# A decode step fed by one stream of weights and caches: the packed array in sixteen lines instead of 128

## The chip, the cores and the metric

The kernel runs on one core of a Trainium2 chip. The metric is the device time of one execution in microseconds (us); less is better. The runs before the change took 375.45, 376.38 and 376.48 us, median 376.38 us.

## The reference: what is computed

One decode step for a batch of two tokens, in float32. The token vector is normalised; one branch is attention over the last 2,048 positions of a key and value cache (32 heads of 128), the other a gated feed-forward block without a nonlinearity. Both are added to the input.

```python
B, D, H, Dh, Sk, F = 2, 512, 32, 128, 8192, 1376
W = min(4096, max(256, Sk // 4))                 # 2048
xn = layernorm(x)
q = (xn @ wq) per head
p = softmax(q . k_cache[:, :, Sk-W:] * Dh**-0.5)
attn = (p . v_cache[:, :, Sk-W:]) @ wo
ffn = ((xn @ w_gate) * (xn @ w_up)) @ w_down
out = x + attn + ffn
```

With one query per head, every byte of cache and weight is used once: the kernel reads 159.47 MB and does little arithmetic with each byte.

## The kernel before, in words

The host packs all inputs but x into one array in device memory, `stream`. It has 128 lines, one for each partition of the on-chip memory; a line holds, load after load, what that partition is to receive. A load is one DMA: it takes a stretch of every line and writes it to the same columns of all 128 partitions of one on-chip tile, `ring` (called `step` in the profile, as the DRAM array is called `in_stream_dram`). `lines()` computes at which element of a line each load starts (a multiple of 128 elements) and how long a line is; its length in units of 128 elements is kept odd. `placed()` gives the column range of each load in `ring`, `loads()` the list of loads.

There are 26 loads. Two small ones, x0 and x1, bring the gate, up and first query weights. Then keys and values of four heads at a time (k0, v0, k1, v1, ...), each 16,384 elements of each partition; between them w1 and w4 with the down-projection, query and output weights. The tail is seven smaller loads: v28, v30, v31, d0, wo7, d1 and d2. All are issued by SyncE (SP), in that order, by `issue(name)`. Keys always go to one region of `ring` and values to another, so the load of the next group's keys waits until TensorE has read the present keys (`issue(f"k{g + 1}")` stands behind `scores(g)`), and likewise for values (behind the loop over `weigh`). While one of the two regions is being read, the load for the other is in flight.

The loop over eight head groups g runs: the query projection (`project`, tile q_ps), the scores (`scores`, s_ps), the maxima and exponentials (`maxima`, `weights`), the weighted values (`weigh`, o_ps), the gathering of heads (`gather`) and the output projection (`wo`, acc). TensorE's program is a hardware loop with waits on semaphores; a load adds 16 to its semaphore when all of it has landed. Every operation is recorded through one helper, so nearly all rows of the profile carry its line, L133.

Of the kernel before, what the change touches and what calls it, by code (L numbers as in the profile page):

```python
# [10 lines left out]
P = 128  # L11
# [41 lines left out]
def loads():  # L53


    v, k = [("v", h) for h in range(H)], [("k", h) for h in range(H)]
    pair = [(("wq", g), ("wo", g - 1)) for g in range(NG)]
    wd = {i: ("wd", i) for i in range(NFC + 1)}
    last = H - HG
    out = {  # L60
        "x0": (None, C_GU, [("gu", GU[0])]),
        "x1": (None, C_GU + GU[0][1], [("gu", GU[1]), ("c", 0)]),
        "k0": ("K", C_K, k[:HG]),
        "v0": ("V", C_V, v[:HG]),
        "w1": (
            None, C_Q[1] - (len(EARLY) - 1) * D - REST,
            [wd[i] for i in EARLY] + [*pair[3], *pair[2], *pair[1]],
        ),
    }
    for g in range(1, NG - 1):  # L70
        out[f"k{g}"] = ("K", C_K, k[g * HG : g * HG + HG])
        out[f"v{g}"] = ("V", C_V, v[g * HG : g * HG + HG])
        if g == 3:
            out["w4"] = (None, C_W, [*pair[4], *pair[7], *pair[6], *pair[5]])
    out["k7"] = ("K", C_K, k[last:])
    halves = [("half", (h, b)) for h in range(last, H) for b in range(B)]
    for name, a, b in (("v28", 0, 4), ("v30", 4, 7), ("v31", 7, 8)):
        out[name] = ({0: "V", 4: "V2", 7: "V3"}[a], C_V + a * W, halves[a:b])
    at = C_K
    for name, ids in (("d0", ROWS), ("wo7", None), ("d1", STRIPS[:-1]), ("d2", STRIPS[-1:])):  # L80
        if ids is None:
            out[name] = ("wo", C_O, [("wo", NG - 1)])
            continue
        out[name] = (None, at, [wd[i] for i in ids])
        at += len(ids) * D
    return out
# [10 lines left out]
def placed():  # L97


    got, spans = {}, {}  # L100
    for name, (_, at, fields) in loads().items():
        lo = at
        for kind, i in fields:
            got[kind, i] = (at, width(kind, i))
            at += width(kind, i)
        spans[name] = (lo, at)
    return got, spans


LINE = 128  # L110


def lines():


    starts, at = {}, 0
    for name, (lo, hi) in placed()[1].items():
        starts[name] = at
        at += -(-(hi - lo) // LINE) * LINE
    return starts, at + LINE * (1 - at // LINE % 2)  # L120


# [320 lines left out]
def build(nc, stream, x_nat, out):  # L443
# [44 lines left out]
    got = {key: ring[:, c : c + w] for key, (c, w) in where.items()}  # L488
    src, tag_of = {}, {}
    starts, total = lines()  # L490
    rows = stream.rearrange("(p i) -> p i", i=total)
    for name, (tag, _, _) in loads().items():
        lo, hi = spans[name]
        src[name] = rows[:, starts[name] : starts[name] + hi - lo]
        tag_of[name] = tag

    def issue(name):
# [30 lines left out]
    total, var, std, rstd = (st[:B, i : i + 1] for i in range(4))  # L528
# [177 lines left out]
    for g in range(NG):  # L706
# [17 lines left out]
        if g == 0:  # L724
# [7 lines left out]
            for i in range(3):  # L732
                part = slice(32 * i, 32 * i + 32)
# [39 lines left out]
def laid_out(x):  # L773

    import numpy as np

    a = x["A_x"].reshape(B, D)
    rows = np.arange(P)
    c = np.zeros((P, CX), a.dtype)
    for n in range(N):  # L780
        c[:, n] = rows % 32 // 4 == n
    for i in range(4):
        c[:, N + i] = rows % 4 == i
        c[:, N + 4 + i] = rows == 32 * i
    for b in range(B):
        c[:, N + 8 + b] = rows % 32 == b
    k, v = (x[name][:, :, SK - W :, :] for name in ("A_k_cache", "A_v_cache"))
    wq = x["A_wq"].reshape(NC, P, H * DH)
    wo = x["A_wo"].reshape(NG, HG, P, D)
    first = [x[name].reshape(NC, P, F) for name in ("B_w_gate", "B_w_up")]  # L790
    first = np.concatenate(first + [wq[:, :, :FB]], axis=2)
    first = np.pad(first, ((0, 0), (0, 0), (0, RUNS * GW - WIDE)))
    wd = x["B_w_down"]

    def field(kind, i):
        if kind == "c":
            return c
        if kind == "half":
            return field("v", i[0])[:, i[1] * W : (i[1] + 1) * W]
        if kind == "k":  # L800
            return k[:, i].transpose(2, 0, 1).reshape(P, CK)
        if kind == "v":
            blocks = v[:, i].reshape(B, NJ, NK, 32, DH)
            return blocks.transpose(1, 3, 0, 2, 4).reshape(P, CK)
        if kind == "wq":
            return wq[:, :, i * FB : (i + 1) * FB].transpose(1, 0, 2).reshape(P, NC * FB)
        if kind == "wo":
            return wo[i].transpose(1, 0, 2).reshape(P, HG * D)
        if kind == "wd":
            w = wd[i * P : (i + 1) * P]  # L810
            if i < NFC:
                return w
            return np.concatenate(
                [w[:, :REST], w[:, REST:].reshape(3, 32, P).transpose(1, 0, 2).reshape(32, REST)]
            )
        runs = first.reshape(NC, P, RUNS, GW).transpose(1, 2, 0, 3).reshape(P, -1)
        return runs[:, i[0] : i[1]]

    starts, total = lines()
    stream = np.zeros((P, total), a.dtype)  # L820
    for name, (_, _, fields) in loads().items():
        at = starts[name]
        for kind, i in fields:
            part = field(kind, i)
            stream[:, at : at + part.shape[1]] = part
            at += part.shape[1]
    return {"stream": stream.ravel(), "x": a}


# [25 lines left out]
```

## Time and profile before

| | |
|---|---|
| median of three runs | 376.38 us |
| the profiled execution's own time | 375.21 us |
| its span on the core | 373.8 us |
| TensorE (PE) busy | 215.1 us, 58% |
| VectorE (DVE) busy | 62.7 us, 17% |
| the loads' DMA queue (q1) busy | 98.9% of 16 DMA engines' span |
| bytes read | 159.47 MB |

The span is what the profiler saw between the first and the last instruction; the execution's own time is 1.41 us longer. "q1" is the queue on which SP's DMAs run, spread over 16 DMA engines; its share is the time that packets took on the sixteen, so 100% means that all sixteen worked all the time. The chain of work that ended last is followed back from the last instruction; "DMA" in it is time in which the chain waited for a load to land.

### The profile page before, as it was taken

To read this page: it belongs to the slowest core of one execution; us is meant where nothing else is said; L and a number is where in the kernel's file an instruction comes from. 1 tells how busy PE (TensorE), PEld (TensorE's weight loads), DVE (VectorE), ACT (ScalarE), POOL (GpSimd) and SP (SyncE) were. 2 spreads that over 40 slices of the span, in tenths; PEclk is the share of its full clock that TensorE was granted. 3 is DMA by queue.
4 is the path that set the end of the run, shared out by engine and by line. 5 is a ranking of instruction groups with operands and counts; after the bars stand their busy time and mean duration, and the time that the engine had idled before them with its cause. 6 is when DMAs were issued, how large, how long until landed. Compare 5 with 4: busy or idle time off the path is not lost.

```text
span 373.8 us, 3210 instructions
## 1 busy us (share of the span) xinstructions
PE 215.1 (58%) x1362; PEld 53.4 (14%) x1362; DVE 62.7 (17%) x161; ACT 15.9 (4%) x31; POOL 15.5 (4%) x38
## 2 busy tenths in 40 slices
PE   0688770097828780776154414637662877095765
PEld 0011110022102110221011100102110211021221
DVE  3000141012120212021202010202120122003203
ACT  5011110000000000000000000000000000000000
POOL 2000000022000200000000200000200020000000
PEclk9989997568986898699869585859896889689999
DMA  8999899999899999989999999899999989999996
GB/s 335 495 449 442 365 428 491 427 449 435 358 442 449 449 449 449 449 351 435 449 449 449 449 449 414 372 449 449 449 449 449 442 365 428 449 449 393 435 419 276
DMA packets 3892, 159.54 MB, mean 427 GB/s; under 512 B 434, under 2 KB 562, under 8 KB 1076
## 3 DMA queue, kind: packets, MB, share of 16 engines
q1 hardware_dynamic: 3888, 159.54, 98.9%
q10 hardware_dynamic: 4, 0.00, 0.0%
HBM read 159.47 MB, written 0.07 MB: 427 GB/s over the span
## 4 chain that ended last, share of the span: by engine, by line
DMA 70%; PE 27%; DVE 1%; ACT 1%; issue 1%; SPq 0%; ACTq 0%
DMA step<-in_stream_dram 70%; PE o_ps L133 14%; PE q_ps L133 8%; PE s_ps L133 3%; PE acc L133 1%; ACT step L133 1%; PE tot L133 1%; DVE qt L133 1%; DVE red L133 0%; DVE om L133 0%; PE pk L133 0%; SPq L133 0%; ACT qz L133 0%; DVE oT L133 0%; ACTq L302 0%
## 5 line engine op out<-in xcount | busy, mean ns | idle before, releaser
L133 PE MATMUL o_ps<-step,p 128*32 128x512 f32 x512 | 71.5, 698 | 57.5 <-DMA step<-in_stream_dram 56.3
L133 PE MATMUL s_ps<-step,qz 128*8 128x512 f32 x512 | 60.6, 628 | 29.1 <-DMA step<-in_stream_dram 22.2
L133 PE MATMUL q_ps<-step,xn 128*2 x112 | 58.7, 674 | 16.5 <-POOL none L133 10.5
L133 PEld LDWEIGHTS o_ps<-step,p 128*32 128x32 f32 x512 | 17.0, 122 | 94.2 <-DMA step<-in_stream_dram 59.8
L133 PEld LDWEIGHTS s_ps<-step,qz 128*8 128x8 f32 x512 | 14.2, 93 | 75.6 <-issue 64.9
L133 POOL COPY step<-step 128x2048 f32<-128x2048 f32 x6 | 11.3, 1889 | 181.9 <-PE acc L133 181.9
L133 PEld LDWEIGHTS q_ps<-step,xn 128*2 128x2 f32 x112 | 9.9, 93 | 61.2 <-issue 61.2
L133 DVE TENSOR_REDUCE mt<-s_ps 128x1 f32<-128x512 f32 x8 | 5.5, 692 | 77.0 <-PE s_ps L133 77.0
L133 PE MATMUL acc<-step,oT 128*2 128x256 f32 x128 | 10.9, 469 | 11.6 <-POOL none L133 8.4
L133 DVE RECIPROCAL rec<-tot 128x8 f32<-128x8 f32 x8 | 1.7, 208 | 73.0 <-PE tot L133 73.0
L133 DVE TENSOR_TENSOR xr<-xr,acc 128x256 f32<-128x256 f32 (+1 forms) x17 | 7.4, 437 | 38.5 <-PE acc L133 38.4
L133 PE MATMUL acc<-step,hT 128*2 128x512 f32 (+1 forms) x10 | 3.3, 995 | 17.7 <-DMA step<-in_stream_dram 17.7
L133 DVE STREAM_TRANSPOSE qt<-q_ps 32x128 f32<-32x128 f32 x28 | 8.6, 306 | 24.8 <-PE q_ps L133 24.5
L133 DVE TENSOR_TENSOR om<-o_ps,cst 128x512 f32<-128x512 f32 x7 | 4.8, 691 | 36.8 <-PE o_ps L133 36.8
L133 PE MATMUL pk<-cst,red 128*128 128x8 f32 x16 | 3.3, 276 | 13.1 <-DVE red L133 13.1
L133 ACT COPY qz<-qt 128x8 f32<-128x8 f32 x8 | 1.6, 204 | 207.9 <-DVE qt L133 207.9
L133 PE MATMUL top<-dg,ones 128*128 128x32 f32 x16 | 3.3, 286 | 10.3 <-DVE dg L133 10.3
L133 ACT ACTIVATE p<-t,zero 128x128 f32<-128x128 f32 x8 | 4.2, 522 | 93.9 <-DVE t L133 93.9
L133 DVE TENSOR_REDUCE red<-om 128x128 f32<-128x512 f32 x7 | 7.1, 1019 | 0.2
L133 DVE TENSOR_TENSOR step<-step 2x1376 f32<-2x1376 f32 x1 | 1.6, 1580 | 32.2 <-ACT step L133 32.2
L133 POOL MEMSET none<- 128x1 f32 x18 | 1.6, 98 | 101.4 <-DMA step<-in_stream_dram 76.9
L133 DVE STREAM_TRANSPOSE sT<-s_ps 128x512 f32<-128x512 f32 x8 | 5.7, 709 | 0.0
(56 smaller groups left out, 55.6 us busy)
## 6 DMA issues: line engine op xcount, KB each, us to landing
step<-in_stream_dram SPq DMA_DIRECT2D x1, 7360.0 KB, 26.7
step<-in_stream_dram SPq DMA_DIRECT2D x1, 5590.5 KB, 17.4
step<-in_stream_dram SPq DMA_DIRECT2D x1, 4096.0 KB, 23.0
step<-in_stream_dram SPq DMA_DIRECT2D x1, 3072.0 KB, 27.7
step<-in_stream_dram SPq DMA_DIRECT2D x2, 1024.0 KB, 25.8
step<-in_stream_dram SPq DMA_DIRECT2D x1, 956.5 KB, 4.6
step<-in_stream_dram SPq DMA_DIRECT2D x1, 768.0 KB, 20.2
step<-in_stream_dram SPq DMA_DIRECT2D x1, 512.0 KB, 23.1
```

What stands on the lines that cost most here:

```text
L133: return getattr(engine, self.method)(*args, **self.kw)
```

## The change

The packed array gets 16 lines instead of 128. A line belongs to eight neighbouring partitions: line q to partitions 8q to 8q+7. Within a line, each load's eight partition rows lie directly behind each other; so a load takes from each line one run of eight rows without a gap. Before, the eight rows were each a line apart (311,680 elements). A load's start in a line is rounded up to 128 elements as before, and a line is 2,491,776 elements long. On the host side the array is filled accordingly. What lands where in `ring` is the same, and so are the number, order, sizes and waits of all loads.

```diff
-LINE = 128
+LINE, SHARE = 128, P // 16

 def lines():
     starts, at = {}, 0
     for name, (lo, hi) in placed()[1].items():
         starts[name] = at
-        at += -(-(hi - lo) // LINE) * LINE
+        at += -(-SHARE * (hi - lo) // LINE) * LINE
     return starts, at + LINE * (1 - at // LINE % 2)
...
     rows = stream.rearrange("(p i) -> p i", i=total)
     for name, (tag, _, _) in loads().items():
         lo, hi = spans[name]
-        src[name] = rows[:, starts[name] : starts[name] + hi - lo]
+        share = rows[:, starts[name] : starts[name] + SHARE * (hi - lo)]
+        src[name] = share.rearrange("q (n i) -> q n i", n=SHARE)
         tag_of[name] = tag
...
     starts, total = lines()
-    stream = np.zeros((P, total), a.dtype)
+    stream = np.zeros((P // SHARE, total), a.dtype)
     for name, (_, _, fields) in loads().items():
-        at = starts[name]
-        for kind, i in fields:
-            part = field(kind, i)
-            stream[:, at : at + part.shape[1]] = part
-            at += part.shape[1]
+        part = np.concatenate([field(kind, i) for kind, i in fields], axis=1)
+        part = part.reshape(P // SHARE, -1)
+        stream[:, starts[name] : starts[name] + part.shape[1]] = part
```

No instruction changes its place on any engine. What changes is the form of the 26 loads on SP. Here is the beginning of SP's program as a difference (- before, + after); the numbers are the destination's dimensions, and the three rows are the loads x0, x1 and k0.

```order
-L133 DMA step<-in_stream_dram 128x1913
-L133 DMA step<-in_stream_dram 128x11181
-L133 DMA step<-in_stream_dram 128x16384
+L133 DMA step<-in_stream_dram 128x1x1913
+L133 DMA step<-in_stream_dram 128x1x11181
+L133 DMA step<-in_stream_dram 128x1x16384
 L334 UNCONDITIONAL_BRANCH
```

Before, source and destination were both 128 rows by n elements. Now the source is 16 by 8 by n, and the destination, still 128 rows, gets a dimension of size one between them so that both sides have three. The other 23 loads change in the same way.

## The prediction

> **What bounds the kernel now.** I read the page's DMA part first, because the kernel uses every byte once.
>
> ```profile
> span 373.8 us, 3210 instructions
> PE 215.1 (58%) x1362; PEld 53.4 (14%) x1362; DVE 62.7 (17%) x161; ACT 15.9 (4%) x31; POOL 15.5 (4%) x38
> DMA packets 3892, 159.54 MB, mean 427 GB/s; under 512 B 434, under 2 KB 562, under 8 KB 1076
> q1 hardware_dynamic: 3888, 159.54, 98.9%
> DMA 70%; PE 27%; DVE 1%; ACT 1%; issue 1%; SPq 0%; ACTq 0%
> ```
>
> The loads' queue keeps sixteen DMA engines busy for 98.9% of 373.8 us, 369.7 us. No compute engine comes near that. The chain of waits agrees: 70% of it is waiting for loads, and its PE pieces run while the next load is already moving. So the kernel lasts as long as its DMA engines need for their bytes, and a change of their rate shows in full.
>
> Next, whether the rate has a ceiling. The table by stretches (columns: the stretch, its length, busy time of each engine, granted clock, DMA share, GB/s):
>
> ```profile
> 113.00:152.00 39.00, 23.73 (x158) 6.12 (x158) 6.53 (x17) 0.72 (x2) 2.08 (x3) 0.81 0.99 430
> 152.00:191.00 39.00, 21.94 (x162) 6.13 (x166) 6.53 (x17) 0.73 (x2) 0.00 (x0) 0.85 0.99 430
> 191.00:249.00 58.00, 25.60 (x162) 6.09 (x161) 6.53 (x17) 0.73 (x2) 2.22 (x5) 0.71 1.00 434
> 249.00:288.00 39.00, 23.24 (x162) 6.11 (x165) 6.53 (x17) 0.73 (x2) 2.09 (x3) 0.85 0.99 430
> 288.00:346.00 58.00, 37.83 (x254) 9.95 (x250) 10.68 (x27) 0.93 (x3) 2.08 (x3) 0.84 0.99 427
> ```
>
> Keys, values and weights land in these stretches, TensorE's load varies from 25.60 of 58 us to 37.83 of 58, and the rate stays between 427 and 434 GB/s: 430/16 = 26.9 GB/s for each engine. That is the signature of sixteen equal fixed lanes, all full, not of a memory that answers unevenly. Reads that come easier therefore have almost nothing to give, and lanes that are used less evenly have everything to take.
>
> **The change part by part.** Bytes, row lengths, destination columns, order and waits stay the same. The term is 0.
>
> Issuing. The three-dimensional form may take SP longer to decode.
>
> ```profile
> L133 SPq DMA_DIRECT2D step<-in_stream_dram x26: 327/328/433, 0.7 to 348.1; - x26
> 1.28 0.53 ACTq L133 DMA_DIRECT2D xr<-in_x_dram x1
> step<-in_stream_dram SPq DMA_DIRECT2D x16, 30.3
> step<-in_stream_dram SPq DMA_DIRECT2D x1, 956.5 KB, 4.6
> ```
>
> SP's 26 issues take 0.328 us (first row: minimum, median, maximum in ns). The dearest issue in this trace is ScalarE's, 0.53 us, so I bound the extra by 0 and 0.2 us each. A load of 8,192 KB (the x16 row) lands 30.3 us after its issue but takes 8.39 MB/430 = 19.5 us to move: it stands about 10.8 us behind another load, and 0.2 us disappears in that. Only the very first issue has no cover: +0.2 us at most, and 26 x 0.2 = 5.2 us if all cover were gone. I take 0.2. A wait is not added, so nothing new queues behind SP.
>
> Reading. Eight rows of a load now lie behind each other instead of 1.25 MB apart. What easier reads could give: x0, 956.5 KB, took 4.6 us to land where 0.98/0.430 = 2.3 us would do. Say all 2.3 us of that came from scattered first reads, which is generous since the same 4.6 us hold the issue and the landing signal: a gain of 0 to 2.3 us. A loss is possible too (sixteen long runs could meet in the memory); no row prices it. I take 0, because behind the start the sixteen lanes are full.
>
> Writing. This is the term that decides. A load is dealt out to the sixteen engines by the outermost rows of its two sides. Before, both sides had 128 rows, so any dealing that is the same on both sides was possible, also one that gives an engine partitions far apart. Now one side has 16 lines and line q holds partitions 8q to 8q+7, so an engine that is dealt a line must write eight neighbouring partitions. If the present dealing was already this one, nothing changes: 0. If it was chosen so that every engine has a way of its own into the on-chip memory, which the level 26.9 GB/s in every stretch suggests, then the new dealing can make two engines write through the same way at the same time while another way is empty. Two on one way of 26.9 GB/s get 13.5 each, and the 369.7 us of transfers become 739.4: +369.7 us. So the bounds are 0 and +369.7.
>
> [...]
>
> How long do two engines stay together? Both carry equal bytes in equal order. While they share, they advance alike, so the distance between them stays what it was at the start; it only helps as a share of half a load, 19.5/2 = 9.75 us. The start scatters by at most the 2.3 us above, 24% of 9.75. A load counts as landed when the slowest pair is done; with eight pairs spread evenly over 0 to 24%, the smallest distance is about 24/9 = 2.7%. I take that: 369.7 x 0.973 = 359.7 us.
>
> The sum, against the profiled execution's own time: 375.2 + 0.2 + 0 + 359.7 = 735.1 us. That execution lies 1.2 us below the median of the runs, 376.38, so I forecast 736 us. All computing hides: PE's 215.1 us fit twice over, and what follows the last landing stays:
>
> ```profile
> 370.76 0.04 issue
> 371.93 0.29 DVE red L133
> ```
>
> The last load lands at 370.76 of 373.8 us: 3.0 us behind it, already in the sum.
>
> **The rivals.** *The pairs drift apart.* If the sharing is not quite even, the distance within a pair grows until one engine writes its first half while the other writes its second; from then on nobody meets. For it: nothing holds them together. Against it: equal bytes, equal rates in every stretch above, and the slowest of eight pairs counts. At best one meeting is paid, 9.75 us: 375.2 + 0.2 + 9.75 = 385 us; at worst it ends where the forecast's own lower end lies, with the whole 24% head start: 375.4 + 0.76 x 369.7 = 656. The middle is 520.
>
> *No meeting: the same time.* The dealing stays what it was, or the ways into the memory are wider than an engine, or the sixteen share a pool that doesn't care who writes where. For it: the level rate would also come from engines that are themselves the limit. Then only 0.2 us of issuing is left: 375.4, or 376.6 as a median. It decides wherever two engines can pass one way at 26.9 GB/s each.
>
> *Faster.* Reading eight adjacent rows takes the start's scatter away: 375.2 - 2.3 = 372.9, or 374.1 as a median. Against it: the queue is at 98.9%, and 2.3 us is the whole of what x0 lost.
>
> **How the numbers follow.** Forecast 0.55, drifting apart 0.28, no meeting 0.14, faster 0.03. The rows show full lanes but not whose they are, hence the 0.14; that nearly two thirds of the rest goes to a lasting meeting follows from the equal rates. The time predicted is the forecast's 736 us, its own range 656 (the full head start) to 760 (the full 744.9 plus 2% for what sharing itself may lose). The range for 8 in 10 has to take in the drifting pairs down to their best, so it is 385 to 760; it leaves out no meeting, faster, and a little of the ends. A measurement of this kernel tells about 0.3% from no change: faster 0.03, same 0.13, slower 0.84 (0.01 of no meeting lies over that bound).
>
> **What would show it.** If right: the queue's share stays near 99% while the mean falls to about 217 GB/s; the stretches show 215 to 225 instead of 430; the sixteen large loads take about 60 us to land; the share of DMA in the chain of waits rises from 70% to about 85%, and PE's busy time stays at 215 us. Drifting pairs would show low GB/s in the early stretches and 430 in the late ones. No meeting: all rows above within a per cent, SP's issues alone longer. What would make it wrong is a way into the on-chip memory that takes two engines at once, or a dealing that still keeps engines apart.

## The result

The changed kernel takes 776.31 us, median of six runs (773.42 to 776.99), against 375.49 us before (median of six, 375.17 to 376.48): 2.066 times as long, 95% interval 2.063 to 2.069. The direction was as forecast, and so, as the experiments show, was the mechanism in the main. The time lies 16 us above the upper end of the range, 760 us, and 40 us above the forecast of 736.

The page of the changed kernel, the lines that answer to those of before:

```profile
span 775.2 us, 3210 instructions
PE 229.9 (30%) x1362; PEld 54.2 (7%) x1362; DVE 62.6 (8%) x161; ACT 15.9 (2%) x31; POOL 15.5 (2%) x38
DMA packets 3892, 159.54 MB, mean 206 GB/s; under 512 B 434, under 2 KB 562, under 8 KB 1076
q1 hardware_dynamic: 3888, 159.54, 99.4%
another core or an unknown queue 65%; PE 21%; DMA 10%; DVE 2%; issue 1%; ACT 0%; SPq 0%; POOL 0%; POOLq 0%; ACTq 0%
```

The number of packets and the bytes are the same to the last digit shown. The sixteen DMA engines are as busy as before, 99.4%, for twice as long: 770.5 us instead of 369.7, a factor of 2.084. The mean rate is 206 GB/s instead of 427. The chain of waits shows one weakness of such a view: most of the waits for loads now stand under "another core or an unknown queue", because the releaser was not matched. There is one core, and the loads are all that is waited for at those places; 65% and 10% together answer to the 70% of before.

The stretches show no ramp (columns as before: the stretch, its length, busy time of each engine, granted clock, DMA share, GB/s), and the issues and landings have their rows too:

```profile
40.00:200.00 160.00, 54.25 (x262) 11.55 (x264) 13.14 (x31) 5.44 (x10) 4.11 (x6) 0.68 0.99 204
200.00:360.00 160.00, 43.72 (x296) 10.99 (x288) 13.05 (x34) 1.45 (x4) 2.09 (x3) 0.66 1.01 209
360.00:520.00 160.00, 34.44 (x216) 8.10 (x212) 8.90 (x24) 1.25 (x3) 2.22 (x5) 0.61 0.99 204
520.00:680.00 160.00, 46.98 (x312) 11.67 (x304) 13.05 (x34) 1.45 (x4) 4.18 (x6) 0.66 1.02 210
L133 SPq DMA_DIRECT2D step<-in_stream_dram x26: 536/536/679, 0.7 to 725.4; - x26
step<-in_stream_dram SPq DMA_DIRECT2D x16, 72.4
```

204 to 210 GB/s from beginning to end: the pairs did not drift apart. An issue on SP takes 0.536 us instead of 0.328.

The trace also holds each DMA packet with its start, duration and size; a packet of 65,536 bytes here is one partition's row of one load (2,048 of them, 128 for each of the sixteen large loads). The records name neither the engine nor the partition; rows are put down to one engine where each starts as the one before it ends, and which partitions it writes is inferred. Rows that follow each other in this way, start in us and duration in ns:

```
before, rows of 65,536 bytes:  120.0:2418 122.4:2418 124.8:2418 127.2:2418 129.7:2418 132.1:2418 134.5:2418
after,  rows of 65,536 bytes:  100.0:5124 105.2:5111 110.3:5118
after,  w1, 58,880 bytes:      115.4:4415 119.8:4600 124.4:4594 129.0:4600 133.6:4422 138.0:4599 142.6:4598 147.2:4599
```

A row took 2.418 us; now most rows take 5.116 (the median of all 2,048 such rows), 2.12 times as long, and none took less than 4.935. In w1's eight rows the first and the fifth are a little quicker (4,415 and 4,422 ns among 4,594 to 4,600). If an engine writes eight neighbouring partitions, the fifth row is where it goes on from its first four to its next four: that would be the halves of a share, with which the forecast counts.

### The profile page after: what moved, and what is told of

The parts are those of the page before. It is cut to its first block, busy times and chain, and to the rows that moved or that the text cites. A ratio compares the mean times of both kernels' runs of the same rounds, so it can differ in the third digit from the quotient of the medians.

```text
span 775.2 us, 3210 instructions
## 1 busy us (share of the span) xinstructions
PE 229.9 (30%) x1362; PEld 54.2 (7%) x1362; DVE 62.6 (8%) x161; ACT 15.9 (2%) x31; POOL 15.5 (2%) x38
## 2 busy tenths in 40 slices
DMA packets 3892, 159.54 MB, mean 206 GB/s; under 512 B 434, under 2 KB 562, under 8 KB 1076
## 3 DMA queue, kind: packets, MB, share of 16 engines
q1 hardware_dynamic: 3888, 159.54, 99.4%
## 4 chain that ended last, share of the span: by engine, by line
another core or an unknown queue 65%; PE 21%; DMA 10%; DVE 2%; issue 1%; ACT 0%; SPq 0%; POOL 0%; POOLq 0%; ACTq 0%
DMA step<-in_stream_dram 10%; PE s_ps L133 6%; PE q_ps L133 6%; PE o_ps L133 6%; PE acc L133 1%; DVE red L133 1%; DVE mt L133 0%; DVE om L133 0%; ACT step L133 0%; PE top L133 0%; PE pk L133 0%; PE tot L133 0%; DVE qt L133 0%; DVE mtt L133 0%
## 5 line engine op out<-in xcount | busy, mean ns | idle before, releaser
L133 PE MATMUL o_ps<-step,p 128*32 128x512 f32 x512 | 75.3, 730 | 197.6 <-DMA step<-in_stream_dram 197.6
L133 PE MATMUL s_ps<-step,qz 128*8 128x512 f32 x512 | 71.3, 720 | 185.3 <-DMA step<-in_stream_dram 185.3
L133 DVE STREAM_TRANSPOSE qt<-q_ps 32x128 f32<-32x128 f32 x28 | 8.6, 306 | 24.8 <-PE q_ps L133 24.6
L133 PEld LDWEIGHTS acc<-step,oT 128*2 128x2 f32 x128 | 3.0, 91 | 37.6 <-POOL none L133 28.9
```

Of the source, the lines that this page charges most:

```text
L133: return getattr(engine, self.method)(*args, **self.kw)
```

## The experiments

**The dealing or the reading?** Theory 1 says that two engines write through one way (one entry into the on-chip memory) at the same time, because each is dealt eight neighbouring partitions. The rivals: long adjacent runs are slow to read, or the three-dimensional form of the loads is slow. Two kernels take the change apart. The first keeps adjacent rows and three dimensions, but in lines of four partitions:

```diff
-LINE, SHARE = 128, P // 16
+LINE, SHARE = 128, P // 32
```

> The array in 32 lines of four neighbouring partitions instead of 16 lines of eight; each load's rows are still adjacent within a line, and the loads are still three-dimensional. Theory 1 (two engines write through the same way into the on-chip memory at the same time because each is dealt eight neighbouring partitions): 32 lines can be dealt so that an engine gets two lines far apart, as in the kernel before, so about 375.5 us (375 to 377) and 430 GB/s in the stretches. Rival 2 (long adjacent runs are read more slowly): runs half as long, still far slower than before, 500 to 776. Rival 3 (the three-dimensional form of the loads is slow): 776.

The second keeps the old layout, in which nothing is adjacent, and changes the dealing alone:

```diff
-    rows = stream.rearrange("(p i) -> p i", i=total)
+    rows = stream.rearrange("(q i) -> q i", i=8 * total + LINE)[:, : 8 * total]
+    rows = rows.rearrange("q (n i) -> q n i", i=total)
...
-        src[name] = rows[:, starts[name] : starts[name] + hi - lo]
+        src[name] = rows[:, :, starts[name] : starts[name] + hi - lo]
...
+    stream = np.pad(stream.reshape(16, -1), ((0, 0), (0, LINE)))
```

> The old layout, every partition's row in a line of its own 1.25 MB from the next, but the loads described as 16 times 8 rows (a gap of 512 bytes after each eight lines keeps them so). Nothing is adjacent; only the dealing to the engines is that of the change. Theory 1: 776 us (765 to 785). Rival 2 (reading of adjacent runs): 375 to 377. Rival 3 (the form): 776 too, told apart by the run with 32 lines.

With 32 lines: 375.76 us, 1.0013 times the kernel before (1.0002 to 1.0023). With the old layout in sixteen shares: 774.29 us, 2.062 (2.059 to 2.066). Two stretches of each, 32 lines first, and the issues with 32 lines:

```profile
113.00:152.00 39.00, 22.91 (x158) 6.05 (x158) 6.53 (x17) 0.73 (x2) 2.08 (x3) 0.85 1.02 440
191.00:249.00 58.00, 25.40 (x158) 6.20 (x158) 6.53 (x17) 0.73 (x2) 2.22 (x5) 0.74 1.00 433
L133 SPq DMA_DIRECT2D step<-in_stream_dram x26: 534/535/651, 0.7 to 349.3; - x26
```

```profile
200.00:360.00 160.00, 48.32 (x308) 11.85 (x304) 13.06 (x34) 1.45 (x4) 2.09 (x3) 0.64 1.01 210
520.00:680.00 160.00, 47.16 (x312) 11.82 (x308) 13.06 (x34) 1.45 (x4) 4.17 (x6) 0.65 1.01 210
```

So neither the form nor adjacency in runs of four rows costs anything that counts, and adjacency gains nothing: what the two slow kernels have in common is the dealing. Two neighbouring lines of the 32 would be the changed kernel's eight partitions; the full rate (440 and 433 GB/s above) speaks against that dealing and for lines further apart, but which lines an engine got no record shows. The form's 0.2 us per issue is there with 32 lines too; 0.49 us of 26 x 0.2 shows in the time. One rival is left open by these two runs: lines of eight rows begin 9.97 MB apart in device memory, lines of four 4.98 MB, so the dealing also settles which places are read at the same time. The next run bears on it.

**Only half of the partitions.** If the ways belong to partitions, a load to 64 of them should be slow without any line of eight:

```diff
-        pr.load("SP", ring[:, lo:hi], src[name], tag=tag_of[name])
+        for part in (slice(0, 64), slice(64, P)) if name in ("w1", "w4") else (slice(0, P),):
+            pr.load("SP", ring[part, lo:hi], src[name][part], tag=tag_of[name])
```

> The kernel before, in its old layout and form; only the loads w1 (7,360 KB) and w4 (8,192 KB) are each issued as two loads of 64 partitions, 0 to 63 and 64 to 127. All sixteen engines take part in each. If partitions 0 to 63 have only half of the ways into the on-chip memory, sixteen engines share eight ways during these loads: the two then take twice as long, 7.54 and 8.39 MB at 430 GB/s once more, 17.5 + 19.5 = 37 us, with 5% for the sharing 41, so 412 to 418 us. If what slows the changed kernel is only that one engine has eight neighbouring partitions, or the reading, or the three-dimensional form, then 375 to 378.

415.92 us, 1.108 (1.106 to 1.111), 40.6 us more than the 375.35 beside it. The stretches 55 to 75 (w1), 113 to 152 (keys and values) and 215 to 260 (w4 among others):

```profile
55.00:75.00 20.00, 0.38 (x2) 0.27 (x2) 1.20 (x4) 0.52 (x1) 0.00 (x0) 0.52 1.10 233
113.00:152.00 39.00, 26.42 (x164) 6.42 (x161) 7.36 (x20) 0.73 (x2) 2.09 (x3) 0.81 0.99 430
215.00:260.00 45.00, 11.97 (x74) 2.86 (x66) 3.95 (x9) 0.20 (x1) 2.22 (x5) 0.64 0.96 256
```

The rate halves while the halves move (233 over a share of 1.10 is 212) and is 430 between them. A row of w1 takes 4.598 us (median), as in the changed kernel. So sixteen engines that write 64 partitions move about 212 GB/s, and the same engines over 128 partitions 430. If the sixteen engines of a load to 64 partitions are dealt four rows each in order, they read 4.99 MB apart, about as with 32 lines, and are slow all the same. That speaks against the distance of the reads as the cause; no run varies the reading alone.

**Eight lines.** With fewer lines than engines, do the engines that get one meet in pairs as well?

```diff
-LINE, SHARE = 128, P // 16
+LINE, SHARE = 128, P // 8
```

> The array in eight lines of sixteen neighbouring partitions. Only eight engines can be dealt a line. If engines were the limit alone: 8 x 26.9 = 215 GB/s, 745 to 780 us, the same as with sixteen lines. [...]

1,424.89 us, in one run. The DMA share is 0.50, which is eight of the sixteen at work, and they move 13.8 GB/s each:

```profile
200.00:600.00 400.00, 53.65 (x332) 13.01 (x336) 14.59 (x38) 1.45 (x4) 6.19 (x9) 0.56 0.50 109
600.00:1000.00 400.00, 62.03 (x408) 15.49 (x400) 17.21 (x44) 1.66 (x5) 4.30 (x8) 0.59 0.50 111
```

Not 745 to 780, which eight free engines would have made: each moves about half of the 26.9 GB/s of one in the kernel before, as Theory 1 has it of engines that meet. Meetings that last would by estimate take twice the changed kernel's 770.5 us of transfers, 1,541 us; the time is 7.5% below that. The typical row is 5.118 us, but some rows grow quicker from stretch to stretch (the mean falls from 4.90 us in the first 200 us to 4.63 behind 1,200); that would fit engines of a pair that come apart a little, but no record names the engine.

**Shifting the pairs in time.** If engines only lose while they are on the same way, setting one of each pair off by half a share should save most of the loss, even though bytes are added. Two loads in front of the first keys are meant to do that (their data are overwritten later); the control gives the same rows to all sixteen, with `(16, 0, P, 5376), (16, 0, P, 5120)`.

```diff
     issue("x1")
+    at = 0
+    for k, base, parts, n in ((12, 0, 96, 5376), (4, 68, 32, 5120)):
+        size = (parts // k) * n
+        take = rows[0:k, starts["k0"] : starts["k0"] + size].rearrange("q (n i) -> q n i", i=n)
+        pr.load("SP", ring[base : base + parts, at : at + n], take)
+        at += n
     issue("k0")
```

> The changed kernel with two more loads in front of the first keys: one on twelve of the engines (8 rows of 21,504 bytes each) and one on four of them (8 rows of 20,480 bytes each), landing where the first values are written later. They add bytes and do nothing else than put engines of a pair apart in time. [...] Theory 1: so 430 to 500 us, 35 to 45% less than the changed kernel though more is loaded, early stretches slow and late ones near 400 GB/s. Rivals 2 and 3, and a sharing that does not depend on when each engine is where: 776 plus the added bytes, 780 to 800.

> Control to the shifted pairs: the two additional loads go to all sixteen engines alike (8 rows of 21,504 and 8 of 20,480 bytes each), so nobody is put apart. Theory 1: 776 plus 336 kB an engine at half of 27.1 GB/s less 5%, 26 us, so 802 us (795 to 810). Rivals: 785 to 802.

Control: 800.66 us (two runs), as theory 1 had it. Shifted pairs: 730.38 us (727.76 to 735.44 in three runs; a fourth took 741.13), 5.9% below the changed kernel and 8.8% below the control, so time apart does help; but 430 to 500 was expected. Those figures were the author's estimate; no run shows which partitions share a way. The stretches of the shifted kernel:

```profile
80.00:120.00 40.00, 10.25 (x66) 2.23 (x66) 2.38 (x7) 0.52 (x1) 0.00 (x0) 0.59 0.99 251
120.00:160.00 40.00, 7.27 (x28) 1.60 (x28) 1.53 (x4) 0.00 (x0) 2.02 (x3) 0.50 1.02 278
160.00:200.00 40.00, 21.34 (x142) 5.07 (x140) 5.13 (x13) 0.20 (x1) 2.08 (x3) 0.78 1.00 226
200.00:360.00 160.00, 47.87 (x318) 12.17 (x318) 14.46 (x39) 1.97 (x5) 2.09 (x3) 0.68 1.00 215
520.00:680.00 160.00, 49.49 (x316) 12.13 (x316) 13.14 (x35) 1.66 (x5) 2.19 (x4) 0.67 1.00 215
```

251 and 278 GB/s while the shift lasts, then 215. Two things stand in the packets. From about 165 us four engines have no packet for 2.4 to 3.6 us: the engines in front had run out of loads, since SP issues the next one (at 166.56 us) only when the last but one has landed on all engines and been read. The lead was not kept in this kernel. And between 96 and 104 us, when groups of engines were at different rows, almost all rows of all sixteen engines took 4.2 to 4.9 us; of the rows that began between 104.5 and 108 us, one for each engine, all took 2.4 to 3.6. A meeting seemed to slow engines that had no part in it. That was a new question.

**Who is slowed by a meeting?** Four kernels add one load in front of the first keys of the kernel before; nothing else changes in it. In one it has 64 partitions, from eight lines of eight rows of 32,768 bytes, and is meant for eight engines that meet in pairs; in the others it has 17, 34 or 68 partitions and is meant for one, two or four engines. With 17 the trace bears the number out: from 45 to 50 us, with the first keys through, the DMA share is 0.06 and the rate 26 GB/s, one engine of sixteen. With 34 the rate falls to 51 GB/s in one slice of the span (112 to 123 us), 1.9 times the 27.1 of an engine that shares nothing; with 68 to 100 (52 to 63 us), 3.7 times, which fits four but is no proof. The diff shows the load for eight engines and, behind the dots, that for one; for two engines its rows are 4:38, for four 4:72.

```diff
+    lo = starts["k1"]
+    flat = bass.AP(stream.tensor, stream.offset + lo, [[16 * total, 8], [FB * P // 8, 8], [1, FB * P // 8]])
+    pr.load("SP", ring[0:64, 0 : FB * P // 8], flat)
...
+    pr.load("SP", ring[4:21, 0 : FB * P // 8], rows[4:21, lo : lo + FB * P // 8])
```

> [...] Question: does a meeting slow only the two engines that meet (first reading) or all sixteen (second reading)? The extra load takes the eight engines 262,144 bytes at half of 27.1 GB/s less 5%, about 20 us, from 18 to 38 us at the latest. First reading: while it lasts the stretch shows 8 x 13 + 8 x 27 = 320 GB/s. Second reading: 16 x 13 = 207 GB/s. The time of the whole is about 375 + 20 = 395 us (388 to 405) by both.

> The kernel before with one more load in front of the first keys: 17 partitions (4 to 20) of 32,768 bytes each. 17 is a prime number, so one engine alone is dealt all of it, 557,056 bytes, while the other fifteen go on with the first keys; the one writes to four partitions after the other that belong to another engine's way, so at any time exactly one way has two engines. First reading (a meeting slows only those who meet): 14 engines at 27 and two at 13 GB/s, 400 GB/s while the first keys move (from 18 to 38 us), then only the one engine at work until about 50 us. Second reading (one meeting slows all sixteen): 16 x 13 = 207 GB/s from 18 to about 60 us. The whole: 375 plus what the one engine is late, 20 to 45 us, by the second reading at its upper end, 415 to 420.

> As with the one engine, but the additional load has 34 partitions (4 to 37), so two engines are dealt 17 rows each, and one or two ways at a time have two engines. If only those who meet are slowed: two to four engines at 13 GB/s and the rest at 27, 375 to 405 GB/s from 20 to 27 us. If the number of meetings decides how far the others are slowed with them (none at one meeting, all at four, as the runs with one and with eight engines showed), something between: 300 to 375.

> [...] If only those who meet are slowed: five engines at 9 to 13 GB/s and eleven at 27, 345 to 360 GB/s from 20 to 27 us. If meetings slow the others too, the more the more there are: 210 to 330.

The times of the whole, one run each, were 395.24 us with eight engines, 405.71 with one, 410.57 with two and 419.56 with four. The stretch 22.6 to 37.5 us, in the order before, one, two, four, eight engines (a stretch counts whole packets, so the rate is to be read beside the share, the number ahead of it):

```profile
22.60:37.50 14.90, 12.77 (x28) 1.95 (x26) 0.00 (x0) 1.61 (x3) 0.00 (x0) 0.98 1.09 471
```

```profile
22.60:37.50 14.90, 12.77 (x29) 1.95 (x26) 0.00 (x0) 1.61 (x3) 0.00 (x0) 0.98 0.99 391
```

```profile
22.60:37.50 14.90, 12.77 (x29) 2.03 (x27) 0.00 (x0) 1.61 (x3) 0.00 (x0) 1.00 1.20 264
```

```profile
22.60:37.50 14.90, 12.06 (x28) 1.95 (x27) 0.00 (x0) 2.15 (x4) 0.00 (x0) 1.00 1.06 222
```

```profile
22.60:37.50 14.90, 12.77 (x29) 2.12 (x27) 0.00 (x0) 1.61 (x3) 0.00 (x0) 0.95 0.95 216
```

By full share that is 432 GB/s before, 395 with one engine, 220 with two, 209 with four, 227 with eight. For two engines at least 300 was expected; that missed. The packets say it row by row (start us : ns; rows of the first keys, 65,536 bytes, unless marked):

```
one engine with the additional load
  the one (32,768 bytes)   18.1:1804 19.9:2461 22.4:2456 24.8:2440 27.3:2407
  whom it meets            18.0:4125 22.2:4864, then 27.5:4609 32.1:4974 on another engine
  any of the others        18.0:2418 20.4:2418 22.8:2418 25.2:2418 27.6:2686 30.3:2680
two engines with it
  whom they meet           18.0:4341 22.3:4920 27.3:5154
  any of the others        18.0:2418 20.4:2418 22.8:3838 26.6:5131 31.8:4874
eight engines with it
  the eight (32,768 bytes) 18.2:2239 20.4:2548 22.9:2554
  the other eight          17.8:4336 22.1:5086 27.2:4788
```

With one engine, the first reading holds: the one and whom it meets drop to half, and the others keep 2.418 us for four rows. After four of its rows (18.1 to 24.8 us) the one goes on to the next four partitions, and at that moment, 27.3 to 27.5 us, the engine that is slowed changes: with the first and fifth rows of w1, the plainest sign in these traces that four neighbouring partitions go together. During this second meeting the others take about 10% longer for two rows, then 2.50 and 2.44 us. With two engines, from 22.6 us on, every engine is slowed, and every row of 65,536 bytes that begins between 26 and 41 us takes 4.7 to 5.2 us. With eight it is the same: 4,336 to 5,086 ns for the other eight too, which have no part in the additional load. Neither reading is right as it stood: one engine with the additional load costs mainly itself and whom it meets (395 GB/s by full share), and with two, four or eight everybody goes at about their pace (220, 209 and 227). How many engines shared a way in the runs with two and four, and which, no record shows; the counts in their expectations are the author's. Whether the reading side has a part in that spreading, and why it sets in at two, no run shows.

## Why the prediction was wrong in its size, point by point

- *What bounds the kernel.* Right. DMA engines 98.9% busy before, 99.4% after; the loss came in full because nothing else is long.
- *Bytes, order, row lengths: 0.* Right: 3,888 packets and 159.54 MB both times.
- *Issuing: at most 0.2 us each, only the first visible.* Right within a few tenths: 0.536 against 0.328 us, and 375.76 against 375.27 us in the kernel with 32 lines, 0.49 us more where 0.2 was taken.
- *Reading: 0.* Right as far as shown: adjacency in runs of four moved nothing (32 lines), and its absence helped nothing (old layout in sixteen shares, 2.062).
- *Writing: the transfers double, +369.7 us.* Right in mechanism as far as shown, mis-sized. That the outermost rows settle the dealing is shown by the old layout in sixteen shares (774.29 us) and by eight lines (a DMA share of 0.50); that two engines can hold each other up, by the run with one additional engine: 2,440 to 2,461 ns for its 32,768 bytes, which take 1,218 in the kernel before, and 4,864 ns for the other's 65,536. The queue's busy time grew by 770.5 - 369.7 = 400.8 us, 31.1 us more than the doubling. In the changed kernel an engine does not get half but less: 65,536 bytes in 5.116 us, 12.8 GB/s where half of a lone engine's 27.1 (65,536 bytes in 2.418 us) is 13.6. The mean row of this size took 5.077 us, 2.097 times 2.421; shorter rows paid less, so the whole queue came to 2.084. The step that failed is the one that took the price of sharing as nothing in the forecast and allowed 2% for it in the upper bound: it is 31.1 of 739.4 us, 4.2%, and 5 to 6% in the long rows. That alone carries the time past 760 us.
- *The head start: 2.7% saved.* This failed too, and in the same direction: the distance within a pair was to be worth 10 us, and not one row of 65,536 bytes ran free. With the 31.1 us this makes the 41 us by which the added transfer time, 359.7 us, fell short. The forecast assumed that a pair apart runs free. The run with two engines shows that this need not be so: from 22.6 us on every engine slowed down, to 220 GB/s by full share. That a distance in one pair therefore buys nothing while other pairs meet is the likely reason; the changed kernel's trace does not show how far apart its pairs were. The eight pairs and the half share of 9.75 us in the forecast are the author's: no run shows which engines make a pair, and what the runs show instead is every long row between 4.935 and 5.136 us and the change after four rows in w1 and in the run with one engine.
- *Drifting apart, 0.28.* Did not happen; 204 to 210 GB/s in the four stretches from 40 to 680 us. Even a shift made on purpose was lost, partly because engines in front ran out of loads at 165 us.
- *No meeting, 0.14, and faster, 0.03.* Out; the run with 32 lines is what no meeting looks like.
- *What would show it.* A share near 99% was as said. The mean rate was 206 GB/s instead of 217, and the stretches lie below 215 to 225. PE's busy time was 229.9 us, not 215, with a granted clock of 0.61 to 0.68 in the stretches, against 0.71 to 0.85 in those of before. Landings of about 60 us were 72.4. Waits for loads, forecast at 85% of the chain, were 75% at most.

The rates by form: a load described as 128 rows on both sides ran at 427 GB/s, one as 32 times 4 at 433 to 440 in the stretches shown, one as 16 times 8 at 206, and all three go to 128 partitions. Which engine wrote which partitions no record says. That engines which meet nobody are slowed as well is what the runs with two, four and eight engines add.

## What to carry to other kernels

How a load's outermost dimension is described can halve its rate; the likely reason is that it decides which engine writes which partitions. Of the forms measured here, 128 rows (375.49 us) and 32 lines of four (375.76) ran at full rate and sixteen times eight (776.31) at half: the bytes and packets look the same, and the DMA engines look as busy. When a DMA-bound kernel shows a full queue at half the rate of another, as here 206 against 427 GB/s, look at the duration of single packets first: here equal bytes took twice the time, so the engines were sharing something and not waiting for work.

## What was not expected of the hardware

Sharing cost more than a fair half: 5.116 us for a row of 65,536 bytes against 2 x 2.418 = 4.836, though the first row of each half of a share took only about 4.95, and some rows of the shifted kernel 4.46. Shorter rows paid less: the median row of 8,192 bytes took 611 ns against twice 314. One engine with an additional load left the engines that met nobody at 2.418 us for four rows; two engines with one took all sixteen to 4.7 to 5.2 us a row, about half their rate. A full DMA queue, 99.4%, is no sign that the engines move what they could.
